# Copying one value product's memory columns out of PSUM earlier, and issuing block 0's softmax after the first segment's small attention

## The chip, the cores and the metric

The kernel runs on one core of one Trainium2 chip. The metric is the device time of one execution, in microseconds (us). A core has five engines with a queue of instructions each: TensorE (PE, matmuls; PEld is its weight load), VectorE (DVE), ScalarE (ACT), GpSimd (POOL) and SyncE (SP, which here issues DMAs). They wait for each other by semaphores. Matmuls write to PSUM, [...]; DVE and ACT copy the results from there to SBUF.

## What is computed

The output is the sum of the input, a memory-augmented attention (A) and a mixing MLP (B), all on the normalised input. Only A matters here. It walks over 64 segments of 32 tokens. Each segment sees its own tokens, causally, and eight memory tokens:

```python
for s in range(n_seg):
    xs = x[:, s * seg_len:(s + 1) * seg_len, :].copy()
    h = jnp.concatenate([mem, xs], axis=1)
    q = jnp.einsum('btd,dhe->bhte', h, Wq)
    k = jnp.einsum('btd,dhe->bhte', h, Wk)
    v = jnp.einsum('btd,dhe->bhte', h, Wv)
    scores = jnp.einsum('bhqe,bhke->bhqk', q, k) * scale
    scores = jnp.where(mask[None, None], scores, -1000000000.0)
    p = _softmax(scores, axis=-1)
    o = jnp.einsum('bhqk,bhke->bhqe', p, v)
    o = jnp.einsum('bhte,hed->btd', o, Wo)
    mem = o[:, :M, :].copy()
    outs.append(o[:, M:, :])
return jnp.concatenate(outs, axis=1)
```

There are 2048 tokens of width 1024, 32 heads of width 128, M = 8 memory tokens and segments of 32. The memory after a segment is its first eight outputs.

## The kernel before

Part B comes first and takes about the first third of the time. The attention then runs in parallel over the segments: the memory that enters each segment is estimated beforehand (MZ), the attention is computed with it, and at the end a comparison (`compare`, `verdict`) says whether the estimates were close enough; if not, a sequential version follows.

**Tiling.** The attention has four blocks `b` of 512 tokens (16 segments) and eight head groups `hg` of four heads; these are 32 steps, i = 8 b + hg, in the loop at L866. A step computes Q, K and V of its head group: `q_chain`, `k_chain` and `v_chain` are chains of eight matmuls of 128 x 512 into one PSUM bank each, followed by a copy to SBUF (L623 on DVE for Q, L635 and L644 on ACT for K and V). A step is twelve places `c`: four Q chains (c = 0 to 3), four K chains (4 to 7), four V chains (8 to 11). In block 0 each K chain is two halves of 260 columns, and each step also projects the memory (`mem_proj`, psM): V's part after c = 11, and Q's at the start of the next step.

**Hooks.** Between these chains stands the rest of the work, for earlier steps: `at(c, f, ...)` puts a function behind place c, in the order of the calls; each engine's queue follows this order, written out by hand. With s the step, p the one before and pp the one before that:

- c = 7: `scores(p)` (64 small matmuls into two banks psS, and two exps on ACT, L669, into ET), `values(pp)`, and `soft(p)`
- `values(pp)`: 60 small matmuls into psO (two tiles of two banks each, "A" and "B") and one into psE (L698), the product of the fourth head of the last four segments, here called the odd one; then DVE adds the memory's part to the first 32 of every 33 columns and writes oX (L702 from psE, eight times L708 from psO)
- `soft(p)`: the softmax, six DVE instructions (L673 transpose, L674 causal mask, L676 sum, L678 reciprocal, L680 product, L682 transpose into PT) and four on POOL (L683 the memory column of PT, L685 BD, L687 SSsum, L688 EM). PT and BD are what `values` reads one step later
- c = 10: `mem_values(pp)`, seven small ACT copies of the 33rd column of each segment (the memory's) to oT: L717 from psE, L721 and L722 from psO
- The first segment has the given memory and is computed apart, for the heads of block 0 (`fz`, eight steps, i = 1 to 8): `first_scores` at c = 4 (POOL), `first_soft` at c = 8 (matmuls into psVZ and psZ, then the small softmax on DVE: L744, L746, L747, the exp L748 on ACT, L749 to L751 into PZ), `first_trans` at c = 11 (psZT reads PZ), `first_values` at c = 1 of the next step
- `make_xm` (L517, DVE): in head groups 5 to 7, three at a time at c = 2, 6 and 10, prepares the next block's input
- `mem_cols` (L657, POOL) at c = 0 writes the memory columns of Q

**PSUM.** psO takes four banks ("A" and "B"). All other tiles of this part (psQ, psK, psV, psM, psS, psE, psVZ, psZ, psZT, psZO) share the tag "mm" with four banks: a new tile takes the bank that has been free longest, in the order of the program, and its first matmul waits for the last reader of the tile before it.

Of the kernel before, what the change touches and what calls it, by code (L numbers as in the profile page):

```python
# [32 lines left out]
SEG = 32  # L33
# [6 lines left out]
W = SEG + 1  # L40
TW = 4 * W
# [22 lines left out]
def kernel(  # L64
# [16 lines left out]
    nc = tc.nc  # L81
# [52 lines left out]
    def mm_tile(name):  # L134
        return psum.tile([P, 512], F32, tag="mm", bufs=4, name=name)

    def aux_tile(shape, tag, name):
        return psum.tile(shape, F32, tag=tag, bufs=1, name=name)
# [250 lines left out]
    with ExitStack() as p3:  # L389
# [107 lines left out]
        def need_w(nm, i):  # L497
            v, hg = A[nm, i]
            A[nm, i] = load_w(v, hg)
# [90 lines left out]
    def hsl(hg):  # L590
        return slice(4 * hg, 4 * hg + 4)

    EMs = {}
    oTs = {}
# [5 lines left out]
    def new_step(i):  # L600
        s = Step()
        s.i = i
        s.b, s.hg = divmod(i, NHG)
        s.Q = qkv.tile([P, 4, 4 * TW], BF16, tag="Q", bufs=2, name="Q")
        if s.hg == 0:
            EMs[s.b] = smp.tile([P, NHG, 4, 4], BF16, tag="EM", bufs=2, name="EM")
            oTs[s.b] = smp.tile([P, H, 16], BF16, tag="oT", bufs=2, name="oT")
        s.xm = A["m", s.b]
        steps[i] = s
        return s  # L610
# [35 lines left out]
    def mem_proj(s, nm, dst):  # L646
        w = A[nm, s.i]
        ps = mm_tile("psM")
        p3_ = ps[:, 0:4 * NZ].rearrange("p (h z) -> p h z", h=4)
        for k in range(KT):  # L650
            for hh in range(4):
                nc.tensor.matmul(p3_[:, hh, :], w[:, k, hh * P:(hh + 1) * P], MZ[:, k, :], start=(k == 0 and hh == 0),  # L652
                                 stop=(k == KT - 1), skip_group_check=True)
        nc.scalar.copy(dst[:, hsl(s.hg), :], p3_)

    def mem_cols(s):
        nc.gpsimd.tensor_copy(s.Q[:].rearrange("p h (s i) -> p h s i", i=W)[:, :, :, SEG], QM[:, hsl(s.hg), 7 + 16 * s.b:23 + 16 * s.b])  # L657
# [32 lines left out]
    def values(s):  # L690
        s.O = [aux_tile([P, 2, 512], t, "psO") for t in "AB"]
        s.E = mm_tile("psE")
        for it in range(15):
            for j in range(4):
                m, hh = divmod(it, 4)
                q = slice(SEG * j, SEG * (j + 1))
                nc.tensor.matmul(s.O[j // 2][:, j % 2, it * W:(it + 1) * W], s.V[q, m, hh * P:(hh + 1) * P], s.PT[q, it, 0:W], start=True, stop=True)  # L697
        nc.tensor.matmul(s.E[:, 0:TW], s.V[:, 3, 3 * P:4 * P], s.BD[:], start=True, stop=True)  # L698
        z = 7 + 16 * s.b
        h0 = 4 * s.hg  # L700
        e3 = s.E[:, 0:TW].rearrange("p (j i) -> p j i", i=W)
        nc.vector.tensor_tensor(oX[:, h0 + 3, 3 * P:4 * P].rearrange("p (j i) -> p j i", i=SEG), e3[:, :, 0:SEG],  # L702
                                VM[:, h0 + 3, z + 12:z + 16].unsqueeze(2).to_broadcast((P, 4, SEG)), op=ALU.add)
        for j in range(4):
            o4 = s.O[j // 2][:, j % 2, 0:15 * W].rearrange("p (t i) -> p t i", i=W)
            for m0, m1, hn in ((1 if s.b == 0 and j == 0 else 0, 3, 4), (3, 4, 3)):
                n = (m1 - m0) * hn
                nc.vector.tensor_tensor(  # L708
                    oX[:, h0:h0 + hn, :].rearrange("p h (m c) -> p m h c", c=P)[:, m0:m1, :, SEG * j:SEG * (j + 1)],
                    o4[:, 4 * m0:4 * m0 + n, 0:SEG].rearrange("p (m h) i -> p m h i", h=hn),  # L710
                    VM[:, h0:h0 + hn, z:z + 16].rearrange("p h (m j) -> p m h j", j=4)[:, m0:m1, :, j].unsqueeze(3).to_broadcast((P, m1 - m0, hn, SEG)), op=ALU.add)

    def mem_values(s):
        h0 = 4 * s.hg
        oT = oTs[s.b]
        e3 = s.E[:, 0:TW].rearrange("p (j i) -> p j i", i=W)
        nc.scalar.copy(oT[:, h0 + 3, 12:16], e3[:, :, SEG])  # L717
        for r in range(2):
            o4 = s.O[r][:, :, 0:15 * W].rearrange("p j (t i) -> p j t i", i=W)[:, :, :, SEG]
            for j in range(2):  # L720
                nc.scalar.copy(oT[:, h0:h0 + 4, :].rearrange("p h (m j) -> p m h j", j=4)[:, 0:3, :, 2 * r + j], o4[:, j, 0:12].rearrange("p (m h) -> p m h", h=4))  # L721
            nc.scalar.copy(oT[:, h0:h0 + 3, 12 + 2 * r:14 + 2 * r].rearrange("p h j -> p j h"), o4[:, :, 12:15])  # L722
# [96 lines left out]
    def load_Rt(b, c):  # L819
        Rt = iop.tile([P, 512], F32, tag="Rt", bufs=2, name="Rt")  # L820
        nc.sync.dma_start(Rt[:], R_v[:, 4 * b + c // 2, (c % 2) * 512:(c % 2 + 1) * 512])
        Rts[b, c] = Rt
# [43 lines left out]
    for i in range(NS):  # L866
        s = new_step(i)
        p = steps.get(i - 1)
        pp = steps.get(i - 2)
        fz = p is not None and p.b == 0  # L870
        last = i == NS - 1
        hooks = {}

        def at(c, f, *a):
            hooks.setdefault(c, []).append((f, a))

        if p is not None:
            at(7, scores, p)
        if pp is not None:
            at(7, values, pp)  # L880
            at(10, mem_values, pp)
        if p is not None:
            at(7, soft, p)
        if 4 < s.hg and s.b + 1 < NB:
            for k in range(3 * s.hg - 15, min(3 * s.hg - 12, KT)):
                at(2 + 4 * (k % 3), make_xm, s.b + 1, (k,))
        if fz:
            at(4, first_scores, p)
            at(8, first_soft, p)
            at(11, first_trans, p)  # L890
        if pp is not None and pp.b == 0:
            at(1, first_values, pp)
        if s.hg == 1 and s.b > 0:
            for c in range(8):
                at(9, out_chain, s.b - 1, c)
        if s.hg == 2 and s.b > 0:
            at(2, norm_sums, s.b - 1)
            for j in range(4):
                at((4, 5, 7, 8)[j], norm_recip, s.b - 1, j)
            at(10, norm_apply, s.b - 1)  # L900
            at(11, norm_add, s.b - 1)
        if s.hg == 3 and s.b > 0:
            at(4, compare, s.b - 1)
            if s.b == 1:
                at(7, compare_first)
        if s.hg == 0 and s.b > 0:
            load_Rt(s.b - 1, 0)
            load_Rt(s.b - 1, 1)
        for c in range(12):
            if c < 4:  # L910
                if c == 0 and s.b == 0:
                    mem_proj(s, "q", QM)
                q_chain(s, c)
                if c == 0:
                    mem_cols(s)
                if c == 3:
                    if i + 1 < NS:
                        need_w("k", i + 1)
                    if s.b == 0:
                        nc.sync.dma_start(wo_sb[:, hsl(s.hg), :], Wo_v[:, hsl(s.hg), :])  # L920
                    if s.hg == 4 and s.b + 1 < NB:
                        load_xT(s.b + 1)
            elif c < 8:
                k_chain(s, c - 4)
                if c == 7 and i + 1 < NS:
                    need_w("v", i + 1)
            else:
                v_chain(s, c - 8)
                if c == 11:
                    if s.b == 0:  # L930
                        mem_proj(s, "v", VM)
                    if i + 2 < NS:
                        need_w("q", i + 2)
            for f, a in hooks.get(c, ()):
                f(*a)
        if last:
            b = s.b
            load_Rt(b, 0)
            load_Rt(b, 1)
            hp = H - 4  # L940
            scores(s)
            values(p)
            soft(s)
            out_part(b, 0, 0, hp)
            mem_values(p)
            out_part(b, 1, 0, hp)
            values(s)
            out_part(b, 2, 0, hp)
            mem_values(s)
            out_part(b, 0, hp, H)  # L950
            out_part(b, 1, hp, H)
            out_part(b, 2, hp, H)
            out_chain(b, 3)
            norm_sums(b)
            for j in range(4):
                norm_recip(b, j)
            norm_apply(b)
            norm_add(b)
            compare(b)
            finite()  # L960
            out_chain(b, 4)
            out_chain(b, 5)
            out_chain(b, 6)
            verdict()
            out_part(b, 7, 0, H, 2)
# [3 lines left out]
    with tc.If(cond > 0):  # L969
        with ExitStack() as fctx:  # L970
# [16 lines left out]
            oTs = fbig.tile([P, H, L], BF16)  # L987
# [107 lines left out]
```

## Time and profile before

| | us, if no unit is given |
|---|---|
| median of three runs | 1499.61 (1498.45 to 1499.66) |
| profiled execution | 1498.22 |
| its span | 1496.5 |
| Q, K and V chains of the attention on PE (L616, L634, L643), busy | 170.4 + 169.7 + 170.5 |
| output projection on PE (L835), busy | 222.2 |
| DVE idle before L702, in all 32 | 217.5 |
| DMA, mean rate | 139 GB/s |
| granted PE clock | 0.999 of full |

A PE busy time is the sum of matmul durations, which overlap in the pipeline. The chain of waits that ended last is 94% PE. In the timeline a line gives start, duration, engine, source line, operation, output and inputs with their shapes, how many instructions were merged, and in brackets the engine's idle time before it with what ended it.

### The profile page before, as it was taken

What the parts mean: (1) busy time and instruction counts of PE and PEld (TensorE: products, weight loads), DVE (VectorE), ACT (ScalarE), POOL (GpSimd) and SP (SyncE); (2) the same over time, 40 slices, a digit from 0 to 9 for tenths busy, and PEclk for the clock granted to TensorE, in tenths of its full rate; (3) what the DMA queues carried; (4) which work ended last, traced back from release to release, by engine and by line L of the source; (5) the groups of instructions that cost most, each with busy time, mean ns of one, the idle gap of its engine ahead of it and who ended that gap; (6) DMA issues with size and microseconds to landing.
All of it is one profiled execution on the core that took longest, in us unless ns stands there. A gap on an engine that the chain in (4) does not pass through costs nothing.

```text
span 1496.5 us, 28334 instructions
## 1 busy us (share of the span) xinstructions
PE 1478.9 (99%) x12432; PEld 760.3 (51%) x12432; DVE 500.8 (33%) x1017; ACT 347.1 (23%) x895; POOL 197.4 (13%) x450
## 2 busy tenths in 40 slices
PE   9999999999999999999999999999999999999998
PEld 7844444444444466565544444444444444444444
DVE  8283010010110213335341355431164442163443
ACT  6633202103012023333220122220123220032220
POOL 6152131211110200101100000000000000000000
PEclk9999999999999999999999999999999999999999
DMA  8599653553121535464531364451245452244301
GB/s 219 137 278 242 250 183 99 185 171 137 64 92 33 207 130 195 142 200 142 181 113 59 98 172 145 144 171 50 83 143 169 154 159 70 67 142 150 119 18 56
DMA packets 189184, 208.39 MB, mean 139 GB/s; under 512 B 50168, under 2 KB 157832, under 8 KB 189056
## 3 DMA queue, kind: packets, MB, share of 16 engines
q1 hardware_dynamic: 180768, 178.82, 39.6%
q0 software_dynamic: 8288, 27.72, 5.3%
q8 instruction: 99, 1.62, 0.5%
q14 instruction: 29, 0.24, 0.1%
HBM read 170.07 MB, written 25.17 MB: 130 GB/s over the span
## 4 chain that ended last, share of the span: by engine, by line
PE 94%; DVE 4%; DMA 1%; issue 0%; SPq 0%; POOL 0%; ACT 0%; DVEq 0%; POOLq 0%; ACTq 0%
PE psK L634 15%; PE psP L835 15%; PE psQ L616 15%; PE ps L553 13%; PE ps L571 13%; PE psV L643 12%; PE ps L366 4%; PE ps L265 2%; PE psS L667 1%; PE psO L697 1%; PE psM L652 1%; DVE oX L708 1%; DVE st L204 1%; PE psvb L425 1%; PE psG L446 1%; DMA x<-in_A_x_dram 0%
## 5 line engine op out<-in xcount | busy, mean ns | idle before, releaser
L835 PE MATMUL psP<-wo_sb,oX 128*128 128x512 bf16 (+1 forms) x1056 | 222.2, 373 | 0.0
L571 PE MATMUL ps<-w,hT_all 128*128 128x512 bf16 x896 | 195.0, 379 | 0.0
L634 PEld LDWEIGHTS <-w 128*128 128x128 bf16 x1280 | 125.1, 98 | 99.1
L643 PE MATMUL psV<-w,xT 128*128 128x512 bf16 x768 | 170.5, 379 | 1.2 <-DVE eZ L744 0.9
L616 PE MATMUL psQ<-xT,w 128*128 128x512 bf16 x768 | 170.4, 379 | 0.0
L634 PE MATMUL psK<-xT,w 128*128 128x512 bf16 x768 | 169.7, 379 | 0.0
L835 PEld LDWEIGHTS <-oX 128*128 128x128 bf16 x1056 | 103.2, 98 | 117.1
L616 PEld LDWEIGHTS <-w 128*128 128x128 bf16 x1024 | 98.8, 98 | 115.9
L635 ACT CAST K<-psK 128x512 bf16<-128x512 f32 (+1 forms) x160 | 80.3, 502 | 303.7 <-PE psK L634 303.7
L623 DVE TENSOR_TENSOR Q<-psQ,QM 128x512 bf16<-128x512 f32 (+1 forms) x128 | 87.3, 685 | 178.8 <-PE psQ L616 111.7
L644 ACT CAST V<-psV 128x512 bf16<-128x512 f32 x128 | 74.9, 592 | 296.2 <-PE psV L643 296.0
L571 PEld LDWEIGHTS <-hT_all 128*128 128x128 bf16 x896 | 87.2, 98 | 103.8
L554 ACT ACTIVATE hT_all<-ps 128x512 bf16<-128x512 f32 x112 | 66.7, 597 | 283.5 <-PE ps L553 283.5
L643 PEld LDWEIGHTS <-xT 128*128 128x128 bf16 x768 | 74.2, 98 | 86.2 <-issue 1.6
L553 PE MATMUL ps<-xn3T,w3a 128*128 128x512 bf16 x448 | 97.7, 379 | 0.0
L553 PE MATMUL ps<-xn3T,w3b 128*128 128x512 bf16 x448 | 97.7, 379 | 0.0
L702 DVE TENSOR_TENSOR oX<-psE,VM 128x128 bf16<-128x128 f32 x32 | 9.3, 292 | 217.5 <-PE psE L698 217.5
L708 DVE TENSOR_TENSOR oX<-psO,VM 128x96 bf16<-128x96 f32 (+2 forms) x256 | 82.0, 392 | 0.0
L841 DVE TENSOR_TENSOR ot<-psP,Rt 128x512 bf16<-128x512 f32 (+1 forms) x33 | 22.3, 675 | 167.7 <-PE psP L835 164.9
L553 PEld LDWEIGHTS <-w3b 128*128 128x128 bf16 x448 | 43.6, 98 | 51.9
L553 PEld LDWEIGHTS <-w3a 128*128 128x128 bf16 x448 | 43.5, 98 | 51.7
L481 DVE TENSOR_SCALAR xt<-xt,lnst 128x1024 bf16<-128x1024 bf16 x16 | 8.7, 546 | 179.4 <-POOL R L480 179.4
(162 smaller groups left out, 1260.9 us busy)
## 6 DMA issues: line engine op xcount, KB each, us to landing
w<-in_A_Wq_dram SPq DMA_DIRECT2D x32, 1024.0 KB, 5.3
w<-in_A_Wk_dram SPq DMA_DIRECT2D x32, 1024.0 KB, 5.3
w<-in_A_Wv_dram SPq DMA_DIRECT2D x32, 1024.0 KB, 6.2
R_scratch<-x POOLq DMA_DIRECT2D x16, 512.0 KB, 7.2
R<-R_scratch SPq DMA_DIRECT2D x16, 512.0 KB, 7.0
chunk<-in_A_Wv_dram SPq DMA_DIRECT2D x8, 1024.0 KB, 5.4
R_scratch<-R POOLq DMA_DIRECT2D x16, 512.0 KB, 4.0
chunk<-in_A_Wo_dram SPq DMA_DIRECT2D x8, 1024.0 KB, 6.3
```

The lines of the kernel that those rows point to most:

```text
L366: nc.tensor.matmul(ps[:], hTB[:, k, o:o + P], w2_sb[:, k, ch * 512:(ch + 1) * 512], start=(k == 0), stop=(k == KT - 1))
L553: nc.tensor.matmul(ps[:], w3[:, k, (f % FH) * P:(f % FH + 1) * P], xn3Ts[tb][:, :, k, :], start=(k == 0), stop=(k == KT - 1))
L554: nc.scalar.activation(h3T[:, f, :], ps[:], ACTF.Gelu_apprx_tanh)
L571: nc.tensor.matmul(ps[:], h3T[:, f, j * P:(j + 1) * P], w4t[f // 4][:, f % 4, ch * 512:(ch + 1) * 512], start=(f == 0), stop=(f == FT - 1))
L616: nc.tensor.matmul(ps[:], w[:, k, hh * P:(hh + 1) * P], s.xm[:, k, 0:512], start=(k == 0), stop=(k == KT - 1))
L623: nc.vector.tensor_tensor(q3[:, j0:16, 0:SEG], p3_[:, j0:16, :], QM[:, 4 * s.hg + hh, z + j0:z + 16].unsqueeze(2).to_broadcast((P, 16 - j0 ...
L634: nc.tensor.matmul(ps[:, 0:c], w[:, k, hh * P:(hh + 1) * P], s.xm[:, k, h2 * c:(h2 + 1) * c], start=(k == 0), stop=(k == KT - 1))
L635: nc.scalar.copy(s.K[:, hh, h2 * c:(h2 + 1) * c], ps[:, 0:c])
L643: nc.tensor.matmul(ps[:], s.xm[:, k, m * P:(m + 1) * P], w[:, k, :], start=(k == 0), stop=(k == KT - 1))
L644: nc.scalar.copy(s.V[:, m, :], ps[:])
L708: nc.vector.tensor_tensor(oX[:, h0:h0 + hn, :].rearrange("p h (m c) -> p m h c", c=P)[:, m0:m1, :, SEG * j:SEG * (j + 1)], o4[:, 4 * m0:4 ...
L835: nc.tensor.matmul(ps[:, 0:w], oX[:, h, m * P:(m + 1) * P], wo_sb[:, h, cc], start=(h == 0), stop=(h == H - 1))
```

## The change

It does two things. The ACT copy of the odd value product's memory columns (L717) moves from `mem_values`, at c = 10, into `values`, behind the DVE add that reads the same bank (L702). And in the eight steps in which the first segment's small attention of block 0 runs, `soft(p)` is issued at c = 11, after `first_trans`, instead of at c = 7, after `values`; in all other steps it stays at c = 7.

```diff
@@ def values(s):
         nc.vector.tensor_tensor(oX[:, h0 + 3, 3 * P:4 * P].rearrange("p (j i) -> p j i", i=SEG), e3[:, :, 0:SEG],
                                 VM[:, h0 + 3, z + 12:z + 16].unsqueeze(2).to_broadcast((P, 4, SEG)), op=ALU.add)
+        nc.scalar.copy(oTs[s.b][:, h0 + 3, 12:16], e3[:, :, SEG])
         for j in range(4):
@@ def mem_values(s):
         h0 = 4 * s.hg
         oT = oTs[s.b]
-        e3 = s.E[:, 0:TW].rearrange("p (j i) -> p j i", i=W)
-        nc.scalar.copy(oT[:, h0 + 3, 12:16], e3[:, :, SEG])
         for r in range(2):
@@ the loop over the steps
         if pp is not None:
             at(7, values, pp)
             at(10, mem_values, pp)
-        if p is not None:
-            at(7, soft, p)
         if 4 < s.hg and s.b + 1 < NB:
...
             at(4, first_scores, p)
             at(8, first_soft, p)
             at(11, first_trans, p)
+        if p is not None:
+            at(11 if fz else 7, soft, p)
         if pp is not None and pp.b == 0:
             at(1, first_values, pp)
```

## The prediction

> **What bounds the kernel now.** I read the page's busy times, then who waited for whom, then one step of block 0 in the timeline, then a step without the bubbles as a measure.
>
> ```profile
> PE 1478.9 (99%) x12432; PEld 760.3 (51%) x12432; DVE 500.8 (33%) x1017; ACT 347.1 (23%) x895; POOL 197.4 (13%) x450
> ```
>
> TensorE is the bound; the other engines matter only where they hold PE up. PE's waits in the attention part, from the waits view (in total, times, longest):
>
> ```profile
> PE psV L643 <- DVE eZ L744: 6.0, 7, 0.9
> PE psV L643 <- ACT V L644: 2.5, 7, 0.4
> ```
>
> Twice in each of seven steps a value chain (eight matmuls into one psV) waits for a PSUM bank. The steps are numbered i = 0 to 31; the seven are i = 2 to 8. The timeline of step 5 (start, duration, engine, line; in brackets the idle time before):
>
> ```profile
> 672.61 1.89 PE L643 MATMUL psV<-w,xm 128*128 128x512 bf16 x8
> 672.81 0.29 DVE L702 TENSOR_TENSOR oX<-psE,VM 128x128 bf16<-128x128 f32 x1 [6.95 <-PE psE L698]
> 673.02 2.46 DVE L708 TENSOR_TENSOR oX<-psO,VM 128x256 bf16<-128x256 f32 x8
> 674.54 0.59 ACT L644 CAST V<-psV 128x512 bf16<-128x512 f32 x1 [1.92 <-PE psV L643]
> 674.56 0.26 PE L742 MATMUL psZ<-KZ,QZ 128*128 128x40 bf16 x4
> 675.15 0.58 ACT L739 CAST VZ<-psVZ 32x512 bf16<-32x512 f32 x1
> 675.18 3.61 PE L643 MATMUL psV<-w,xm 128*128 128x512 bf16 x16 [0.35 <-ACT V L644]
> 675.40 0.70 DVE L673 STREAM_TRANSPOSE EQ<-ET 128x512 f32<-128x512 f32 x1
> 679.32 0.27 DVE L744 SCALAR_TENSOR_TENSOR eZ<-psZ,c_mask_sb 40x160 f32<-40x160 f32 x1
> 679.64 1.89 PE L643 MATMUL psV<-w,xm 128*128 128x512 bf16 x8 [0.85 <-DVE eZ L744]
> 680.42 0.34 ACT L748 ACTIVATE eZ<-eZ 40x160 f32<-40x160 f32 x1 [4.69 <-DVE eZ L747]
> 680.78 1.07 ACT L644 CAST V<-psV 128x512 bf16<-128x512 f32 x2
> 681.42 1.06 PE L652 MATMUL psM<-MZ,w 128*128 128x71 bf16 x27
> ```
>
> Call the four value chains V8 to V11. In the built program the "mm" banks of this step go: psE 3, V8 5, psVZ 4, psZ 2, V9 5, V10 4, V11 2, psM 5. psE keeps bank 3 until mem_values has copied its memory columns after V10, so only three banks turn. V9 (675.18) therefore waits for V8's own copy (674.54 + 0.59); V11 (679.64) waits for psZ's bank, which L744 reads at 679.32, because the whole softmax (675.40 to 679.39) stands ahead of L744 on DVE. ACT sits 4.69 us in front of the small exp L748 with V9's copy behind it, which is why psM, on V9's bank, is late too.
>
> The same stretch of step 1, where no value product is open:
>
> ```profile
> 568.71 0.26 PE L742 MATMUL psZ<-KZ,QZ 128*128 128x40 bf16 x4
> 568.81 5.34 PE L643 MATMUL psV<-w,xm 128*128 128x512 bf16 x24
> 573.99 1.23 PE L652 MATMUL psM<-MZ,w 128*128 128x71 bf16 x32
> ```
>
> Here psZ to V9 takes 0.10 us and the three chains follow at 1.73 each: no wait.
>
> [...] the matmuls read 379 ns each but start every 216 (1.73 / 8). So the idle column starts too late, and I count from start to start. [...] A psE at 619.63 sits idle 1.53 us with no releaser, and the instruction queue moved two packets in that stretch while the DMA engines were nine tenths busy. I take it as such a fetch; the trace doesn't prove it.
>
> **The change part by part.**
> *What goes, start to start.* psZ to V9: 0.62 against 0.10, so 0.52. V9 to V11: 4.46 (679.64 - 675.18) against 2 x 1.73 = 3.46, so 1.00. V11 to psM: 1.78 against 1.73, so 0.05. Together 1.57. Check by whole periods: step 5 to 6 takes 26.46 from psS to psS (671.38 to 697.84); step 1 takes 24.28 and lacks psO and psE, which take 0.62 (671.99 to 672.61): 24.90, a difference of 1.56. Steps 2 to 7: 6 x 1.56 = 9.4. Step 8 has no psM; its gaps are 0.52, 1.01, then 0.34 before psZT (759.85 - 757.78 - 1.73) and 0.09 before the next psQ: 1.96. Sum 11.3 us.
>
> *psE's memory columns copied at once.* The copy (0.18 us, ACT) now stands after the two exps of psS and before V8's copy, and waits for L702 on DVE. In step 5: L702 ends at 673.10, the copy at about 673.3. Behind it on ACT is V8's copy, not ready before 674.5: cover 1.2 us. In front of L702 DVE has been idle 6.95 us (in total 217.5 us over the 32), so the wait doesn't grow in blocks 1 to 3 either: there too L702 ends at 853.29 and the V copy comes at 854.73. The banks now turn by four: V9 takes psE's, V10 V8's, V11 psVZ's, psM psZ's. Without bubbles V9 would start at 674.66 (bank free at 673.3), V10 at 676.39 (V8's copy ends 675.13), V11 at 678.12 (psVZ's copy ends 675.73), psM at 679.85. The smallest margin is 1.26 us. Blocks 1 to 3 show no PE wait on a bank (their steps are 22.05 us, PE busy throughout), so the freer ring gains nothing there.
>
> *The softmax moved behind the small attention, block 0, eight steps (i = 1 to 8).* On DVE six instructions (L673 to L682, 3.99 us) go behind the small softmax (2.3 us from L744 to L751) and, in steps 5 to 7, behind make_xm (0.68). L744 starts when the adds of L708 end, 675.4; the exp on ACT comes at about 676.4 (ACT's psVZ copy ends at 675.73), before V9's copy is due, PZ at 677.8, while psZT needs it at 680.9. Then the softmax runs to 681.8, or 682.4 behind make_xm. Queued behind it on DVE is the next step's first Q add (L623). That step starts at 683.64 - 1.57 = 682.07, and L623 comes 2.2 us after a step's start (659.38 - 657.18): 684.3. Cover 1.9 to 2.5 us. If it were gone, the first Q bank is wanted again by the fourth Q chain, 5.3 us into the step, another 2.4 us of slack. Of the softmax's four POOL instructions L685 to L688 end by some 683.4 instead of 680.4; they pass nothing on POOL, and mem_cols behind them would slip under 1 us. Its Q columns, PT and BD are read by scores and values of the next step at the earliest, some 14 us later. No DMA moves; SP's queue is as before. Cost 0.
>
> *Unknown.* The one 1.53 us fetch gap may stay or fall elsewhere: 0 taken, 1.5 less as the low end. On the other side, if the idle column (6.0 + 2.5 + 0.2) were the true loss, 8.7 instead of 11.3.
>
> **Sum.** The profiled execution took 1498.22 (span 1496.5 and 1.7 around it): minus 11.3 is 1486.9. The median of the three runs, 1499.61, lies 1.4 above it: 1488.3 is my forecast.
>
> **The rivals.**
> B: the first bubble stays, because V9 now waits for two engines in a row (DVE's add, then ACT's copy) instead of V8's copy. Against it: 1.36 us of margin. It would keep 7 x 0.52 = 3.6: 1491.9.
> C: the second bubble stays, because another reader holds the bank that V11 gets (psVZ's copy behind something on ACT). Against it: 2.4 us of margin. Only 3.6 us gained: 1496.0.
> D: no change, because PE's slack is taken up by the weight loads in the shorter steps. Each step of block 0 loads 4 MB; 160 GB/s becomes 170. For it: the DMA engines are at half their time in a step. Against it: a load lands 5.3 us after its issue and is wanted some 24 us later. 1499.6.
> E, slower: the softmax, now last on DVE, runs into the next step and holds the Q adds until the fourth Q chain finds no bank. It decides once the softmax ends more than 4.6 us (2.2 + 2.4) after the step's start, about 5 us later than worked out; at one chain (1.73) in each of eight steps it costs 13.8: 1488.3 + 13.8 = 1502.1. The only thing that could delay it so is the round trip to ACT for the exp, 0.46 us of DVE idle now.
>
> **How the numbers follow.** Forecast 0.82, B 0.09, C 0.03, D 0.03, E 0.03. The forecast's own range: 1498.45 (lowest run) - 11.3 - 1.5 = 1485.6 up to 1499.66 - 8.7 = 1491.0; taking in B, 1485.6 to 1492.0. Since 0.2% is 3.0 us, about what can be told from no change, forecast, B and C count as faster: 0.94; D as same 0.03; E as slower 0.03.
>
> **What would show it.** Right: PE's two waits on psV are gone from the waits view; psZ to V9 is 0.10; a block 0 step takes 24.9 us from psS to psS; ACT's idle time before the small exp is under 1 us; steps of blocks 1 to 3 still take 22.05. Wrong: a new wait of psV on the oT copy (B) or on VZ (C), of psQ or psK on Q's add (E), or of PE on a weight's DMA (D). The forecast fails if a block 0 step stays above 25.5 us.

## The result, and the profile after

| | us |
|---|---|
| before, four runs | 1499.03 (1498.44 to 1499.66) |
| changed, four runs | 1487.39 (1486.88 to 1489.14) |
| ratio | 0.9924, 95% interval 0.9907 to 0.9942 |

The change saves 11.6 us (8.7 to 13.9 by the interval); 11.3 had been forecast. From the waits view of the changed kernel, PE's waits in the attention part (in total, times, longest):

```profile
PE psE L698 <- issue: 1.8, 1, 1.8
PE psO L697 <- issue: 0.2, 1, 0.2
```

Both waits of psV on a bank are gone. What is left is the single gap before psE, which was there before (1.5 us), and a small one in step 5; both come back in the last section. The chain of waits says the same: DVE had 4% of the span in it, now 0% (before, then changed).

```profile
PE 94%; DVE 4%; DMA 1%; issue 0%; SPq 0%; POOL 0%; ACT 0%; DVEq 0%; POOLq 0%; ACTq 0%
PE 98%; issue 1%; DMA 0%; SPq 0%; DVE 0%; ACT 0%; POOL 0%; ACTq 0%; POOLq 0%
```

The timeline of step 5, the step that the prediction took apart (the change moves the line numbers: the early copy is L704 here, the small softmax L743 to L750):

```profile
670.24 1.89 PE L643 MATMUL psV<-w,xm 128*128 128x512 bf16 x7
670.44 0.29 DVE L702 TENSOR_TENSOR oX<-psE,VM 128x128 bf16<-128x128 f32 x1 [7.28 <-PE psE L698]
670.77 0.16 ACT L704 CAST oT<-psE 128x4 bf16<-128x4 f32 x1 [0.80 <-DVE oX L702]
672.17 0.59 ACT L644 CAST V<-psV 128x512 bf16<-128x512 f32 x1 [1.24 <-PE psV L643]
672.19 0.26 PE L741 MATMUL psZ<-KZ,QZ 128*128 128x40 bf16 x4
672.30 5.34 PE L643 MATMUL psV<-w,xm 128*128 128x512 bf16 x24
673.03 0.31 DVE L743 SCALAR_TENSOR_TENSOR eZ<-psZ,c_mask_sb 40x160 f32<-40x160 f32 x1
674.13 0.34 ACT L747 ACTIVATE eZ<-eZ 40x160 f32<-40x160 f32 x1 [0.78 <-DVE eZ L746]
675.05 0.32 DVE L750 TENSOR_TENSOR PZ<-eZ,mxZ 40x160 bf16<-40x160 f32 x1
675.89 0.70 DVE L673 STREAM_TRANSPOSE EQ<-ET 128x512 f32<-128x512 f32 x1
677.47 1.23 PE L652 MATMUL psM<-MZ,w 128*128 128x71 bf16 x32
679.17 0.71 DVE L682 STREAM_TRANSPOSE PT<-Pn 128x512 bf16<-128x512 bf16 x1
679.70 2.97 PE L616 MATMUL psQ<-xm,w 128*128 128x512 bf16 x12
681.90 0.66 DVE L623 TENSOR_TENSOR Q<-psQ,QM 128x480 bf16<-128x480 f32 x1 [2.02 <-ACT Q L622]
```

From psZ to V9 is 0.11 us (672.19 to 672.30), and the three chains run through to psM in 5.17 (3 x 1.73). The copy ends at 670.93, 1.4 us before V9 wants the bank. The exp waits 0.78 us in ACT's queue, not 4.69. The softmax ends at 679.88, 0.2 us into the next step, and the first Q add behind it still finds DVE idle for 2.02 us. In the built program the banks of this step now go psE 3, V8 5, psVZ 4, psZ 2, V9 3, V10 5, V11 4, psM 2: four banks in turn, as the prediction had it.

The stages view gives each step from psS to psS (its length, then PE's busy time, PE's weight loads, DVE, ACT and POOL, the granted PE clock, the DMA share and GB/s). Steps 2 and 3 before, then steps 2, 3 and 4 of the changed kernel:

```profile
590.41:616.87 26.46, 25.25 (x334) 16.29 (x333) 10.65 (x25) 9.14 (x32) 2.97 (x11) 1.00 0.49 160
616.87:644.92 28.05, 25.31 (x335) 16.37 (x334) 10.65 (x25) 9.14 (x32) 2.97 (x11) 1.00 0.47 152
590.47:615.36 24.89, 24.79 (x334) 16.23 (x335) 10.63 (x25) 9.52 (x32) 2.86 (x11) 1.00 0.53 169
615.36:643.79 28.43, 26.48 (x333) 16.89 (x335) 10.72 (x25) 9.53 (x32) 2.87 (x11) 0.94 0.48 149
643.79:668.67 24.88, 24.77 (x332) 16.20 (x333) 11.82 (x27) 9.52 (x32) 2.86 (x11) 1.00 0.73 209
```

A step that took 26.46 us takes 24.89. Steps of blocks 1 to 3 take 22.05 as before (in block 1, psS at 842.52 and 864.57). Step 3 is the exception, 28.43: it has the gap of 1.84 us, and after it a lower PE clock. That is enough to make this profiled execution, 1489.14, the slowest of the four: step 3 has 3.54 us over its neighbours here, 1.59 in the profile before (28.05 over 26.46). Less the difference of 1.95, 1489.14 is 1487.2, beside the other three runs.

### The profile page after: what moved, and what is told of

Same layout as the page of the kernel before. It is cut to its first block, busy times and chain, and to the rows that moved or that the text cites. A ratio compares the mean times of both kernels' runs of the same rounds, so it can differ in the third digit from the quotient of the medians.

```text
span 1487.4 us, 28224 instructions
## 1 busy us (share of the span) xinstructions
PE 1471.0 (99%) x12314; PEld 760.3 (51%) x12432; DVE 500.6 (34%) x1017; ACT 352.0 (24%) x895; POOL 195.9 (13%) x450
## 3 DMA queue, kind: packets, MB, share of 16 engines
q8 instruction: 99, 1.62, 0.5%
## 4 chain that ended last, share of the span: by engine, by line
PE 98%; issue 1%; DMA 0%; SPq 0%; DVE 0%; ACT 0%; POOL 0%; ACTq 0%; POOLq 0%
PE psK L634 15%; PE psV L643 15%; PE psP L834 15%; PE psQ L616 15%; PE ps L553 13%; PE ps L571 13%; PE ps L366 4%; PE ps L265 3%; PE psS L667 1%; PE psO L697 1%; PE psM L652 1%; PE psvb L425 1%; PE psG L446 1%; PE ps L294 0%; DMA x<-in_A_x_dram 0%
## 5 line engine op out<-in xcount | busy, mean ns | idle before, releaser
L702 DVE TENSOR_TENSOR oX<-psE,VM 128x128 bf16<-128x128 f32 x32 | 9.3, 291 | 218.2 <-PE psE L698 218.2
```

## The experiments

The kernels ran in three groups, each beside the kernel before: the changed kernel again, the two halves and the one with 48 places (before: 1498.34 us in 13 runs); then the early copy in block 0, the softmax later still, 12 places and the V load (before: 1498.96 in nine); then the changed kernel a third time and 30 places (before: 1499.15 in nine). A ratio is to the kernel before of the same group.

**The changed kernel again.**

> The changed kernel once more, as the reference for the runs beside it. Both theories: 11.6 us under the kernel before, as measured. In its profile a block 0 step from psS to psS takes 24.9 us, and step 3 is longer by the gap before psE (1.84 us in the first profile).

Measured: 1486.84 us, ratio 0.9919 (0.9906 to 0.9933), 11.5 us gained (10.0 to 14.1 by the interval). The steps take 24.89 us, the gap before psE is 1.74.

**The early copy alone.** Against the changed kernel:

```diff
+        if p is not None:
+            at(7, soft, p)
...
-        if p is not None:
-            at(11 if fz else 7, soft, p)
```

> The early copy alone; block 0's softmax stays at c = 7. My theory (two separate waits): V9 and V11 no longer wait, since they get psE's and psVZ's banks, but the small softmax still stands behind the big one on DVE, so psZT now waits for PZ, about 0.75 us in steps 2 to 7 and 1.8 us in step 8. Block 0 step about 25.7 us, gain 6 x 0.76 + 0.15 = 4.7 us: 1494.3. Rival 'the freer ring is all': 11.6 us gained, 1487.4. Rival 'the order on DVE is all': nothing gained, 1499.0.

Measured: 1494.98 us, ratio 0.9973 (0.9963 to 0.9983). Neither rival: 3.4 us gained (2.5 to 5.5 by the interval). The waits view of this kernel names the wait that took the place of the old ones:

```profile
PE psZT L755 <- DVE PZ L750: 5.6, 7, 1.7
```

In its timeline of step 5 the chains run through, but ACT's exp and DVE's PZ are as late as ever:

```profile
674.11 5.34 PE L643 MATMUL psV<-w,xm 128*128 128x512 bf16 x24
678.77 0.27 DVE L743 SCALAR_TENSOR_TENSOR eZ<-psZ,c_mask_sb 40x160 f32<-40x160 f32 x1
679.87 0.34 ACT L747 ACTIVATE eZ<-eZ 40x160 f32<-40x160 f32 x1 [4.70 <-DVE eZ L746]
681.16 0.27 PE L755 MATMUL psZT<-c_ident_sb,PZ 128*128 128x40 bf16 x4 [0.65 <-DVE PZ L750]
```

The step takes 25.79 us (25.7 expected), step 8 takes 24.45 instead of 24.53. That is 6 x 0.67 + 0.08 = 4.1 us, beside 4.7 expected. So a freer ring moves the wait from V11 to psZT: PE first misses a bank, then, with the bank there, the data.

**The later softmax alone.** Against the changed kernel:

```diff
-        nc.scalar.copy(oTs[s.b][:, h0 + 3, 12:16], e3[:, :, SEG])
@@ def mem_values(s):
+        e3 = s.E[:, 0:TW].rearrange("p (j i) -> p j i", i=W)
+        nc.scalar.copy(oT[:, h0 + 3, 12:16], e3[:, :, SEG])
```

> The softmax at c = 11 alone; psE's columns are copied at c = 10 as before. My theory: V9 still waits for V8's own copy (0.52 us by starts, 0.35 in the idle column), V11's wait and the late psM go. Block 0 step about 25.4 us, gain 6 x 1.05 + 1.44 = 7.7 us: 1491.3. Rival 'the freer ring is all': nothing gained, 1499.0. Rival 'the order on DVE is all': 11.6 us gained, 1487.4.

Measured: 1490.32 us, ratio 0.9947 (0.9933 to 0.9960): 8.0 us gained (6.0 to 10.0), 7.7 expected; a step takes 25.40. In its waits view one of the two old lines stands untouched, the other is gone; in step 5 V9 starts 0.62 us after psZ, and the exp no longer waits for long:

```profile
PE psV L643 <- ACT V L644: 2.5, 7, 0.4
```

```profile
671.32 0.26 PE L742 MATMUL psZ<-KZ,QZ 128*128 128x40 bf16 x4
671.94 5.34 PE L643 MATMUL psV<-w,xm 128*128 128x512 bf16 x24 [0.36 <-ACT V L644]
673.26 0.34 ACT L748 ACTIVATE eZ<-eZ 40x160 f32<-40x160 f32 x1 [0.77 <-DVE eZ L747]
```

The two parts alone save 3.4 and 8.0, together 11.4, against 11.5 for both at once in the same group, with intervals of 3 to 4 us. The steps in the profiles are sharper: in steps 2 to 7 the parts save 0.67 and 1.06 against 1.57 for both, in step 8 0.08 and 1.45 against 1.96. So for the most part they remove different waits, but not wholly: 0.16 us of a step is gained by either, and 0.43 us in step 8 by the two together alone.

**The early copy in block 0 only.**

```diff
-        nc.scalar.copy(oTs[s.b][:, h0 + 3, 12:16], e3[:, :, SEG])
+        if s.b == 0:
+            nc.scalar.copy(oTs[s.b][:, h0 + 3, 12:16], e3[:, :, SEG])
@@ def mem_values(s):
+        if s.b > 0:
+            e3 = s.E[:, 0:TW].rearrange("p (j i) -> p j i", i=W)
+            nc.scalar.copy(oT[:, h0 + 3, 12:16], e3[:, :, SEG])
```

> The changed kernel, but with the early copy in block 0 only; in blocks 1 to 3 psE's columns are copied at c = 10 as before. My theory: the gain lies wholly in block 0, so the time is that of the changed kernel (1486.8 in the last runs, within 1 us) and a step of blocks 1 to 3 still takes 22.05 us. Rival: the freer ring also helps in blocks 1 to 3; then the time is higher by more than 2 us.

Measured: 1487.85 us, ratio 0.9928 (0.9914 to 0.9941). The interval reaches down to a gain of 8.8 us, so the time alone does not rule out a loss of over 2 us; the profile does. A step of block 1 is 22.05 us (psS at 840.80 and 862.85), as with the early copy. Blocks 1 to 3 neither gain nor lose by it.

**The softmax later still.** This was meant to force rival E.

```diff
-        if p is not None:
-            at(11 if fz else 7, soft, p)
+        if p is not None and not fz:
+            at(7, soft, p)
         if pp is not None and pp.b == 0:
+            at(2, soft, pp)
```

> The prediction's slower rival E, forced: block 0's softmax is issued later still, behind the third Q chain of the next step (c = 2). My reckoning: the softmax starts when the third Q's add has ended, about 6 us into the step, and holds the fourth Q's add (due at 7.1) until about 10.0; the last bank wanted of the four is then late by about 1.0 us, in each of eight steps: 8 us over the changed kernel, about 1495, with a PE wait on Q's add (L623). If DVE's lateness cost a whole chain a step, as E was priced: 13.8 us, 1500.6. If the softmax is free anywhere before it is read: 1486.8.

Measured: 1487.45 us, ratio 0.9933 (0.9919 to 0.9946): no cost that shows. My reckoning of 8 us was wrong. The fourth Q's add was indeed late, as the timeline shows for step 5, whose Q chains start at 652.61:

```profile
654.81 0.66 DVE L623 TENSOR_TENSOR Q<-psQ,QM 128x480 bf16<-128x480 f32 x1 [6.53 <-ACT Q L622]
659.62 7.26 PE L634 MATMUL psK<-xm,w 128*128 128x260 bf16 x64
659.82 0.19 ACT L622 CAST Q<-psQ 128x32 bf16<-128x32 f32 x1 [1.54 <-PE psQ L616]
662.70 0.71 DVE L682 STREAM_TRANSPOSE PT<-Pn 128x512 bf16<-128x512 bf16 x1
663.34 0.62 DVE L623 TENSOR_TENSOR Q<-psQ,QM 128x480 bf16<-128x480 f32 x1
```

The softmax ends 10.8 us into the step. The fourth Q's add, which could have followed its ACT part at 660.01, starts at 663.34 and ends at 663.96, while the K chains run on unbroken. The built program says why. In the changed kernel the fourth Q's bank goes to the fourth K half. Here the fourth Q lies in bank 4, and the K halves take 3, 5, 2, 3, 5, 2 and only then 4: the seventh half, which starts some 6 x 0.90 us after 659.62, at 665.0. So the banks do not turn in a fixed order: here the bank that comes free late is given out late, and the program is built with this order.

But this is not yet E. Here three Q adds stand ahead of the softmax on DVE, and the first starts at 654.81, 2.2 us into the step, as without the change; so the first Q's bank was free in time for the fourth Q chain, which takes it in this program too. A softmax that holds the first Q add was not run.

**What the gap before psE is.** Three kernels move PE's instructions by 2 x N places, with N matmuls of one column at the start (they are not used); a fourth moves a load:

```diff
+                for i in range(N):
+                    nc.tensor.matmul(ps[:, 0:1], fill[:, 0:P], fill[:, 0:1], start=True, stop=True)
```

N = 24:

> The changed kernel with 24 one-column matmuls more at the start (48 PE instructions), which are not used. It tests what the gap before psE in step 3 is. If it belongs to a place in PE's instruction stream that comes every 256 instructions (in the first profile a 0.22 us gap in step 5 lies 1278 instructions, 5 x 256 less 2, after it), it leaves step 3 and shows before psE in step 6, whose place is then 196 modulo 256 (195 in step 3 so far). If it belongs to the DMA traffic of step 3, it stays in step 3. Time as the changed kernel plus at most 1.5 us for the added matmuls.

N = 6:

> The changed kernel with six one-column matmuls more at the start, not used, which move every later PE instruction by 12 places. If the gap before psE in step 3 comes from place 195 to 196 of 256 in PE's instruction stream, no psE of block 0 stands there now, the gap of 1.7 us goes or shrinks, and the time is 1.5 to 3 us under the changed kernel, about 1485 (more where the PE clock also drops after the gap). If the gap only moves along, 1486.8 to 1487.3.

N = 15, beside the changed kernel once more:

> The changed kernel with 15 one-column matmuls more at the start, not used, so that PE's later instructions move by 30 places. Place 195 of 256 then lies 30 before psE in step 3 and at least 17 away from psE in all other steps of block 0. If the gap shrinks with the distance from psE (1.7 us at 0, 0.94 at 12 places, none at 48 so far), it is under 0.5 us here, and the time is 1 to 1.5 us under the changed kernel. If some place always shows it, no difference.

> The changed kernel, as the reference for the run beside it: about 11.5 us under the kernel before, with the gap of 1.6 to 1.8 us before psE in step 3.

The load of V's weights in step 3 issued later, by ACT:

```diff
-                if c == 7 and i + 1 < NS:
+                if c == 7 and i + 1 < NS and i != 3:
                     need_w("v", i + 1)
...
                 v_chain(s, c - 8)
+                if c == 8 and i == 3:
+                    need_w("v", i + 1, nc.scalar)
```

> The changed kernel with one load moved: in step 3 the next step's V weights (1 MB) are issued from ACT behind V8's copy instead of from SP at the end of the K chains, so that no load runs while PE stands at the place of the gap. If the gap in step 3 needs DMA traffic beside it, it goes: about 1485. If the place in the instruction stream is enough, it stays 1.5 to 1.8 us: 1486.8.

| kernel | where the gap stands in block 0 | gap, us | time, us | ratio to before, interval |
|---|---|---|---|---|
| changed (third time) | psE, step 3 | 1.85 | 1488.29 | 0.9927 (0.9913 to 0.9941) |
| 12 places | six psO matmuls before psE, step 3 | 0.94 | 1488.51 | 0.9931 (0.9917 to 0.9945) |
| 30 places | 15 psO matmuls before psE, step 3 | 0.85 | 1487.26 | 0.9915 (0.9901 to 0.9928) |
| 48 places | psE, step 6 (and 0.8 at a psV in step 4) | 1.85 | 1488.42 | 0.9929 (0.9914 to 0.9944) |
| V load later | psE, step 3 | 1.93 | 1488.47 | 0.9935 (0.9919 to 0.9950) |

A matmul here is two instructions, its weight load and itself (the profile before has 12432 of each). The gap is the idle time, as the profile has it. With 12 and 30 places added the gap lies exactly 6 and 15 matmuls earlier, as the timelines show (the number of matmuls after the gap ends the line):

```profile
618.42 0.22 PE L699 MATMUL psO<-PT,V 32*128 32x33 bf16 x6 [0.94 <-issue]
```

```profile
618.49 0.27 PE L699 MATMUL psO<-PT,V 32*128 32x33 bf16 x15 [0.85 <-issue]
```

With 48 it leaves step 3 and appears in step 6, as forecast from the count modulo 256; the one in step 4 stands at the same place modulo 256. So the gap belongs to a place in PE's instruction stream, and not to the V weights' load, which was moved behind it and left it at 1.93. Two expectations failed. With 30 places the gap was to be under 0.5 us and is 0.85. The time gain of 1.5 to 3 us expected from 12 places did not come, and of 30 places it can't be told: the intervals overlap. In the profiles step 3 takes 26.00 and 25.88 us with 12 and 30 places, against 26.58 to 26.87 in the four profiles with both edits in block 0, the whole gap and a full clock: 0.6 to 1.0 us, less than these runs can tell.

## Why the prediction was right

- *The two bubbles and their size.* Right. Start to start, 1.56 per step was forecast and 26.46 - 24.89 = 1.57 measured; in step 8, 1.96 and 1.96 (24.53 to 22.57; psS at 742.42 and 764.99 now). That the times agree to 0.3 us is in part luck, as their interval is wide; it is the steps that confirm the sum, 6 x 1.57 + 1.96 = 11.4. The idle column's sum, 8.7, would have been 3 us short: it starts from the ends of matmuls that read 379 ns each and start every 216, and counting from starts was what made the number.
- *Which edit removes which.* The prediction priced the bubbles, not the two edits apart. The two halves do: the copy ends V9's wait (0.52) and gives V11 a bank; the softmax's place ends the late small softmax, which held V11's bank and, once that was free, psZT's data.
- *The copy waits for DVE at no cost.* Right: L702 starts 0.3 us after psE, the copy ends 0.5 us after it, and V8's copy behind it on ACT is not due for another 1.2 us. Rival B had a margin of 1.36; 1.37 is measured (670.93 to 672.30).
- *The softmax at the end of the step at no cost.* Right, with 2.0 us of cover left in step 5 (1.9 forecast behind make_xm).
- *Rival E's price and point.* Not tested. E was to decide when the first Q add is held beyond 4.6 us into the step. In the one run with a later softmax the first three adds came ahead of it, and only the fourth was 3.3 us late. What failed there is the reckoning made for that run, 8 us by a fixed turn of four banks, and with it the description of the ring given ahead of the prediction: a tile does not always take the bank that has been free longest in the order of the program.
- *Rivals B, C, D.* None came: no PE wait on the copy, on psVZ's copy or on a weight.
- *The one gap, taken to stay at its size.* That it is a fetch was an estimate, from two packets of the instruction queue. It stayed, 1.5 to 1.9 us in every profile of a kernel that leaves PE's instruction count ahead of it as it was. That the PE clock could fall after it was not in the sum. In the profiled execution step 3 had 1.95 us more over its neighbours than before, 0.3 of it by the gap and 1.6 by the clock.

## What to carry to other kernels

DVE took its work in the order of the program here: before, in step 5, psZ was complete at 674.82, and L744, which reads it, started at 679.32, behind the six instructions of the softmax. In such an order a short chain that the bottleneck waits for belongs ahead of a long one that nobody needs for another step; here the same instructions in another order were worth 8.0 us by themselves. A PSUM tile that is kept for one late small read takes a bank out of the ring for that whole time: before, in step 5, psE's for 9.4 us, from 672.54 to the end of this copy.

```profile
681.74 0.18 ACT L717 CAST oT<-psE 128x4 bf16<-128x4 f32 x1
```

Where the bottleneck waits for a bank, read it at once; in blocks 1 to 3, where it did not wait, the same early copy gained nothing (22.05 us a step with it and without). And a stall on TensorE is counted from start to start against the same stretch without it, since in these traces the idle column starts from ends that lie past the next start (379 ns against 216).

## What the runs showed that I had not expected

The gap before psE moves with PE's instruction count, 256 places being one turn: with 48 places the gaps in steps 4 and 6 are 1278 instructions apart, and so are those in steps 3 and 5 of the changed kernel. The instruction queue q8 moved 99 packets and 1.62 MB, 16 KB each, and PE's 2 x 12432 instructions are some 97 turns; from these two counts I estimate that a packet brings PE one turn. In the changed kernel one packet starts between 615.8 and 616.0 us (the DMA view of these 0.2 us):

```profile
q8 instruction: 1, 0.02, 29.3%
```

That is while PE runs psS and psO, 248 instructions in 1.2 us, nearly a whole turn; PE resumes at 618.43, some 2.5 us later. In the profile before, the packet starts between 617.0 and 617.2 and PE resumes at 619.63, again 2.5 later. (It is one of the two packets that the prediction counted; the other starts after the gap, and in the gap itself the DMA engines were seven tenths busy, not nine.) It is much the same wherever the DMA view was taken at such a gap: with the V load later the packet starts at 615.6 and PE resumes at 618.23, with 30 places it is 615.8 and 618.49, and at the 0.2 us in step 5 of the changed kernel 667.5 and 669.89, 2.4 to 2.7 us each. The reading that fits, an estimate and no more, is that PE came to the end of a turn before the next one was there. In step 18, in block 2, psE stands at nearly the same place (196 modulo 256, 195 in step 3) and shows no gap; there a packet starts between 1070.6 and 1070.8, and psE comes at 1075.57, 4.8 us after it. Why some packets start so late was not tried. The distance to the end of the small matmuls alone does not set the gap: it is 1.85, 0.94 and 0.85 us at 0, 12 and 30 places, none in step 3 at 48, but the one in step 4 ends 5.3 us behind psE.

After this gap PE's clock can fall. In the first profile V8's eight matmuls took 2.48 us instead of 1.73, and weight loads were 0.43 us apart until 622.8 (0.22 otherwise); the clock granted in 617 to 622 us was 0.74. Of the three profiles of the changed kernel, all with this gap, two show such a fall (in the second the clock was 0.75 from 622 to 627 us), and the third, of an execution of 1486.61 us, shows none. Of the other nine only that with 48 places does, behind its gap in step 6. From psE to psVZ behind the gap the three profiles with a fall take 2.54, 3.35 and 3.41 us, and the nine without one 1.78 to 1.80. The length of the gap alone does not decide: from psS to psE, with the gap, it is 3.07, 2.97 and 3.08 us in the three, and 3.16 with the V load later, without a fall.

The fall in the first profile is to half the clock, for 3.41 us. The stages view, with the time ahead and behind (the clock is the third number from the right):

```profile
616.02:619.42 3.40, 1.50 (x66) 1.08 (x67) 0.73 (x4) 0.79 (x3) 0.25 (x1) 1.00 0.84 241
619.43:622.83 3.40, 3.40 (x17) 1.51 (x16) 2.88 (x10) 1.16 (x2) 0.00 (x0) 0.50 0.23 73
622.85:626.25 3.40, 3.40 (x17) 1.55 (x16) 2.79 (x6) 1.33 (x3) 0.00 (x0) 1.00 0.00 0
```

In the clock records of the trace it lasts 3.413 us and starts 614.40 us after the first record, which is 180 times 3.4133. The profiles before and after each have one more fall, in their last 1.5 us; these start 1488.211 and 1481.385 us after the first record, 436 and 434 times 3.4133. So the clock seems to be set in stretches of this length; this is my estimate, from three falls in two traces. In the stretch just ahead of the fall, from 616.02 to 619.43, psS, psO and the gap fill 2.4 us. In the profile before, counted off in the same way, a border at 617.73 divides them into 0.9 and 1.9 us, and there is no fall. So it may be a matter of where the gap falls in such a stretch. That rests on two traces, and no run moved the borders.
